# Half 1's softmax on a Trainium2 core: exponentials, sums and reciprocals issued one mixing round later

## The chip, the cores and the metric

The kernel runs on one core of one Trainium2 chip. Five engines work side by side, each with its own queue of instructions that it takes in order: TensorE (PE in the profile; its weight loads are PEld), VectorE (DVE), ScalarE (ACT), GpSimd (POOL) and SyncE (SP), which here issues most of the transfers. They wait for each other through semaphores. The metric is the device time of one execution in microseconds (us).

## The reference

The input `x` has 2048 tokens of 512 values, in bf16. It is normalised per token (`xn`), and two branches are computed from `xn` and added to `x`. Constants are cut out below.

```python
def _A_ref(x, wqkv, wo):                 # attention: 32 heads of 16, 8 taps, 2 tokens apart
    q, k, v = split(x @ wqkv)
    idx = pos[:, None] - 2 * arange(8)[None, :]
    logits = einsum('bhsd,bhswd->bhsw', q, k[idx]) * Dh ** -0.5
    logits = where(idx >= 0, logits, -1e9)
    attn = softmax(logits, axis=-1)      # over the 8 taps
    o = einsum('bhsw,bhswd->bhsd', attn, v[idx])
    return merge_heads(o) @ wo

def _B_ref(x, w_in, w_sp, b_sp, w_out):  # gated mixing over tokens
    z = gelu(x @ w_in)                   # 1376 columns
    z1, z2 = z[..., :688], layernorm(z[..., 688:])
    g = einsum('ts,bsf->btf', w_sp, z2) + b_sp[None, :, None]
    return (z1 * g) @ w_out

xn = layernorm(x)
return x + _A_ref(xn, A_wqkv, A_wo) + _B_ref(xn, B_w_in, B_w_sp, B_b_sp, B_w_out)
```

## The kernel before

The 2048 tokens are 16 tiles of 128. For the attention they are also two halves of 1024 (`hb` 0 and 1). Within a half, the 128 partitions hold 32 heads for each of four token groups, and 256 tokens of a group lie along a row. The order of the work is written out by hand: instructions stand in each engine's queue in the order in which the program issues them, and a transfer goes into the queue of the engine that issues it.

The first part (to about 67 us of the profile) normalises `x`, computes the `z2` half of the GELU for all tiles (line 241 on TensorE, 248 on ScalarE), and q, k and v. VectorE multiplies q by shifted k (`products`, line 344) and folds the channels (`fold`, 351); TensorE sums over them with a selection matrix (`head_sums`, 363), and ScalarE writes the logits to `a_sb` (`reduce_heads`, `reduce_two`: lines 369 and 375). `a_sb` holds 8 taps by 512 columns per partition: columns 0 to 255 are half 0, the others half 1.

**A softmax** of one half has five steps. `softmax_top` takes the maximum over the taps and subtracts it (VectorE, lines 382 to 385). `softmax_exp` is one ScalarE instruction on the whole half (388). `softmax_sums` adds the eight taps in three VectorE instructions (393 to 395) into the scratch tile `s4`. `softmax_recip` makes the reciprocal of the sums on ScalarE as Exp of minus Ln (399 and 400) into `r1`. `softmax_norm` multiplies the half by it on VectorE (404). ScalarE loads a table of functions (ACT_TABLE_LOAD) where the next instruction's function is not in the one at hand; a load carries the line of the instruction that it serves.

**The mixing rounds** are the second part. Round `j` has `mix(j)`, 32 matmuls of a row tile of `w_sp` with all of `z2` (line 576), whose result `pg` ScalarE evicts with the bias to `gs` (579), and `z1_tile(j)`, eight matmuls into `pz` (588), which ScalarE evicts through the GELU to `z1b` (592). From round 4 on, `pg` and `pz` come from one pool of two buffers (`ps_a`; the call `bank_pair(name, j > 3)` excludes the other). So the `pg` of a round can start only when `gs` has emptied the `pg` of the round before, and the same holds for `pz`. `mix` also issues the transposing load of `w_sp` for round `j + 5` on SyncE (411; `wspT` has five buffers). `gate_out(j)` multiplies `gs` by `z1` on VectorE (597), and SyncE sends the product through a transposing transfer into `uT` (598). `z1b` and `gs` have three buffers each.

**VectorE's own stream** runs beside these rounds. `av_ops` is a generator: for each quarter of 128 columns it multiplies `v` by the weights in four products (657), adds them (662, 664) and writes the quarter of `op` (666). After two quarters, which are half 0, it calls `softmax_norm(1)`, and goes on with half 1. `vector_work(4.6)` takes instructions from it until their stated times exceed 4.6 us. So a round of the loop from 691 on issues, in this order: `mix`, `z1_tile`, some of the products, and `gate_out(j - 1)`, with the steps of half 1's softmax at places fixed by `j`.

**The end.** `out_b` multiplies `uT` by `w_out` (line 746, six matmuls a tile), `out_a` multiplies `op` by `w_o` in row-tiled matmuls (755, 56 for each quarter `jj`), both into `po`; `store` adds `x` on VectorE (762) and SyncE writes the tile out. Fourteen of a head's 16 channels go through `op`; the two others are copied into unused rows of `uT` (`op_rest`, line 646, for half 1 from ScalarE's queue).

Of the kernel before, what the change touches and what calls it, by code (L numbers as in the profile page):

```python
# [47 lines left out]
def kernel(  # L48
# [328 lines left out]
    def softmax_top(hb):  # L377
        l = lg[hb]
        if hb == 0:
            V.tensor_tensor(l[0:32, :, 0:HALO], l[0:32, :, 0:HALO], mask[:], ALU.add)  # L380
        m4 = s4[:, 0].bitcast(BF16).rearrange("p a (b t) -> p (a b) t", b=2)
        V.tensor_tensor(m4, l[:, 0:4, :], l[:, 4:8, :], ALU.max)
        V.tensor_tensor(m4[:, 0:2, :], m4[:, 0:2, :], m4[:, 2:4, :], ALU.max)
        V.tensor_tensor(m4[:, 0, :], m4[:, 0, :], m4[:, 1, :], ALU.max)
        V.tensor_tensor(l, l, m4[:, 0, :].unsqueeze(1).broadcast_to([P, W, TG]), ALU.subtract)

    def softmax_exp(hb):
        A.activation(lg[hb], lg[hb], ACT.Exp)

    def softmax_sums(hb):  # L390
        hsl = slice(hb * TG, (hb + 1) * TG)
        halves = [a_sb[:, w:w + 4, hsl].rearrange("p (a b) t -> p a b t", b=2) for w in (0, 4)]
        V.tensor_tensor(s4[:], halves[0], halves[1], ALU.add)
        V.tensor_tensor(s4[:, 0], s4[:, 0], s4[:, 1], ALU.add)
        V.tensor_tensor(s4[:, 0, 0], s4[:, 0, 0], s4[:, 0, 1], ALU.add)

    def softmax_recip(hb):

        A.activation(s4[:, 0, 0], s4[:, 0, 0], ACT.Ln)
        A.activation(r1[:], s4[:, 0, 0], ACT.Exp, scale=-1.0)  # L400
# [171 lines left out]
    def mix(j):  # L572
        pg = bank_pair("pg", j > 3)
        for k in range(NT):
            for hh in range(2):
                PE.matmul(pg[:, hh, 0:FHALF], wsps[j][:, k, :], z2[:, k, hh * FHALF:(hh + 1) * FHALF],  # L576
                          start=(k == 0), stop=(k == NT - 1))
        gs = gsp.tile([P, 2, FHALF], BF16, name="gs")
        A.activation(gs[:], pg[:, :, 0:FHALF], ACT.Identity, bias=b_col[:, j:j + 1])  # L579
        if j + 5 < NT:  # L580
            load_wsp(j + 5)
        gss[j] = gs

    def z1_tile(j):
        pz = bank_pair("pz1", j > 3)
        for hh in range(2):
            for kc in range(C):
                PE.matmul(pz[:, hh, 0:FHALF], xnT[:, kc, j * P:(j + 1) * P],  # L588
                          w_z1[:, kc, hh * FHALF:(hh + 1) * FHALF],
                          start=(kc == 0), stop=(kc == C - 1))  # L590
        z1 = z1b[j % 3]
        A.activation(z1[:, 0:FH].rearrange("p (a b) -> p a b", a=2), pz[:, :, 0:FHALF], ACT.Gelu_apprx_tanh)  # L592
        z1s[j] = z1

    def gate_out(j):
        gs, z1 = gss.pop(j), z1s.pop(j)
        V.tensor_tensor(z1[:, 0:FH], gs[:].rearrange("p a b -> p (a b)"), z1[:, 0:FH], ALU.mult)
        SP.dma_start_transpose(uT[:, :, j * P:(j + 1) * P], z1[:])
# [43 lines left out]
    def op_rest(hb, q):  # L642

        for k in range(NG):
            for e in range(2):
                q.dma_start(uT[64 + 32 * e:96 + 32 * e, MCH - 1, hb * SB + k * TG:hb * SB + (k + 1) * TG],
                             op[32 * k:32 * k + 32, DHA + e, hb * TG:(hb + 1) * TG])
# [26 lines left out]
    def vector_work(us):  # L674
        while us > 0:
            t = next(work, None)
            if t is None:
                return
            us -= t
# [4 lines left out]
    def load_xr(jj):  # L684
        xr = xrp.tile([P, NG, D], BF16, name="xr")
        SP.dma_start(xr[:], x_g[jj // 2, jj % 2])
        xrs.append(xr)
# [3 lines left out]
    for j in range(4, NT):  # L691
        if j > 4:
            mix(j)
            z1_tile(j)
        if j == 8:
            softmax_recip(1)
        vector_work(4.6)
        if j == 6:
            softmax_top(1)
            softmax_exp(1)  # L700
        if j == 7:
            softmax_sums(1)
        gate_out(j - 1)
        if j == 5:
            SP.dma_start(wout[:, 0:MCH - 1, :], B_w_out[0:(MCH - 1) * P, :].rearrange("(m p) n -> p m n", p=P))
            SP.dma_start(wout[0:FTAIL, MCH - 1, :], B_w_out[(MCH - 1) * P:FH, :])
            for e in range(2):
                SP.dma_start(wout[64 + 32 * e:96 + 32 * e, MCH - 1, :],
                             A_wo.rearrange("(h d) n -> d h n", d=DH)[DHA + e])
        if 6 <= j < 10:  # L710
            k = j - 6
            SP.dma_start(wo_r[32 * k:32 * k + 32, :, :], A_wo.rearrange("(h d) n -> h d n", d=DH)[:, 0:DHA, :])
        if 11 <= j < 13:
            load_xr(j - 11)
        if j == 13:
            op_rest(0, SP)
# [96 lines left out]
```

## Time and profile before

| | |
|---|---|
| median of three runs | 201.62 us (200.99 to 202.24) |
| the profiled execution | 201.13 us, its span 199.4 us |
| granted TensorE clock in the span | 1.0 |
| mixing matmuls, line 576 | 512, mean 309 ns |
| products of VectorE, line 657 | 16, mean 2287 ns |
| the exponential, line 388 | 2 (one a half), mean 1911 ns |
| a table load on ScalarE | 1283 ns each, on every line |
| Ln and Exp of the reciprocals, lines 399 and 400 | 2 each, mean 417 and 418 ns |
| `gs`, line 579; GELU of `z1`, line 592 | 16 each, mean 832 and 744 ns |

The durations come from the one profiled execution. "Idle before" in a row is the time in which the engine stood still ahead of the instruction, followed by what released it. A group such as "x32" in the timeline is a run of like instructions that are merged: its first start and the time to the end of the last. Busy time in four stretches of the mixing rounds (from, to; then busy us and number of instructions for each engine, granted clock, mean busy share of the DMA engines, GB/s):

```profile
105.00:115.00 10.00, 10.00 (x71) 6.69 (x70) 9.86 (x9) 4.05 (x5) 0.00 (x0) 1.00 0.93 192
115.00:125.00 10.00, 9.39 (x66) 6.20 (x64) 9.86 (x9) 6.71 (x8) 0.00 (x0) 1.00 0.93 178
125.00:135.00 10.00, 10.00 (x70) 6.70 (x69) 9.96 (x7) 6.25 (x8) 0.00 (x0) 1.00 1.06 190
135.00:145.00 10.00, 10.00 (x71) 6.72 (x69) 9.93 (x8) 1.82 (x4) 0.00 (x0) 1.00 0.94 172
```

The columns of engines are PE, PEld, DVE, ACT and POOL. The mixing matmuls of rounds 5 to 9 start at 98.36, 104.20, 110.04, 116.64 and 122.47 us.

### The profile page before, as it was taken

What the parts mean: (1) busy time and instruction counts of PE and PEld (TensorE: products, weight loads), DVE (VectorE), ACT (ScalarE), POOL (GpSimd) and SP (SyncE); (2) the same over time, 40 slices, a digit from 0 to 9 for tenths busy, and PEclk for the clock granted to TensorE, in tenths of its full rate; (3) what the DMA queues carried; (4) which work ended last, traced back from release to release, by engine and by line L of the source; (5) the groups of instructions that cost most, each with busy time, mean ns of one, the idle gap of its engine ahead of it and who ended that gap; (6) DMA issues with size and microseconds to landing.
All of it is one profiled execution on the core that took longest, in us unless ns stands there. A gap on an engine that the chain in (4) does not pass through costs nothing.

```text
span 199.4 us, 3851 instructions
## 1 busy us (share of the span) xinstructions
PE 194.2 (97%) x1558; PEld 120.0 (60%) x1564; DVE 178.7 (90%) x208; ACT 105.0 (53%) x151; POOL 18.5 (9%) x65
## 2 busy tenths in 40 slices
PE   7999999999999999999999989999999999999994
PEld 7655555556666666666566656666666664444442
DVE  4899979999999999999999999999999999954083
ACT  4778987668898999496632575932133330000000
POOL 3045640002220020200100000000000000000000
PEclk9999999999999999999999999999999999999999
DMA  6984834998999239999899898999864222017632
GB/s 166 322 288 81 185 72 89 163 260 181 186 188 190 38 32 210 241 218 130 183 198 169 210 207 166 180 181 193 169 153 136 58 41 43 0 43 194 219 120 90
DMA packets 68770, 30.86 MB, mean 155 GB/s; under 512 B 57248, under 2 KB 67344, under 8 KB 68624
## 3 DMA queue, kind: packets, MB, share of 16 engines
q1 hardware_dynamic: 66976, 25.24, 58.3%
q0 software_dynamic: 1360, 5.24, 14.2%
q8 instruction: 12, 0.20, 0.4%
q10 hardware_dynamic: 416, 0.14, 0.3%
q14 instruction: 6, 0.05, 0.1%
HBM read 9.79 MB, written 2.10 MB: 60 GB/s over the span
## 4 chain that ended last, share of the span: by engine, by line
DVE 44%; PE 44%; issue 6%; POOL 3%; ACT 2%; DVEq 0%; ACTq 0%
PE pg L576 19%; DVE pr L344 15%; PE po L746 10%; PE po L755 6%; DVE pr L351 6%; PE pz L588 5%; DVE stats L197 2%; DVE pw L657 2%; DVE pw L662 2%; DVE qk L344 2%; DVE z L276 2%; PE idle L102 2%; DVE xn L202 1%; PE pzb L241 1%; DVE zst L259 1%
## 5 line engine op out<-in xcount | busy, mean ns | idle before, releaser
L576 PE MATMUL pg<-z,wspT 128*128 128x344 bf16 x512 | 77.1, 309 | 0.6 <-ACT gs L579 0.6
L576 PEld LDWEIGHTS <-wspT 128*128 128x128 bf16 x512 | 50.0, 98 | 25.7 <-issue 1.2
L657 DVE TENSOR_TENSOR pw<-vp,a_sb 128x4096 bf16<-128x4096 bf16 x16 | 36.3, 2287 | 0.1
L579 ACT ACTIVATE gs<-pg,b_col 128x688 bf16<-128x688 f32 x16 | 13.3, 832 | 38.7 <-PE pg L576 38.7
L344 DVE TENSOR_TENSOR pr<-qk 128x8192 bf16<-128x8192 bf16 (+1 forms) x8 | 30.9, 3882 | 0.0
L588 PE MATMUL pz<-w_z,xnT 128*128 128x344 bf16 x128 | 21.3, 309 | 0.0
L241 PE MATMUL pzb<-w_z,xnT 128*128 128x344 bf16 x128 | 19.8, 309 | 0.2 <-ACT xnT L226 0.2
L746 PE MATMUL po<-wout,uT 128*128 128x512 bf16 x88 | 19.3, 379 | 0.2 <-issue 0.2
L662 DVE TENSOR_TENSOR pw<-pw 128x4096 bf16<-128x4096 bf16 x8 | 18.3, 2289 | 0.1
L241 PEld LDWEIGHTS <-xnT 128*128 128x128 bf16 x128 | 12.4, 98 | 6.7 <-ACT xnT L226 0.4
L588 PEld LDWEIGHTS <-xnT 128*128 128x128 bf16 x128 | 12.4, 98 | 6.3 <-issue 0.3
L294 ACT CAST qk<-pq 128x1024 bf16<-128x1024 f32 x12 | 12.1, 1012 | 5.8 <-PE pq L291 5.8
L351 DVE TENSOR_TENSOR pr<-pr 128x2048 bf16<-128x2048 bf16 (+1 forms) x10 | 15.1, 1538 | 0.1
L746 PEld LDWEIGHTS <-uT 128*128 128x128 bf16 x90 | 8.7, 98 | 10.7 <-issue 0.4
L316 PE MATMUL pv<-xnT,wv 128*32 128x512 bf16 x256 | 14.4, 380 | 0.0
L592 ACT ACTIVATE z1b<-pz 128x688 bf16<-128x688 f32 x16 | 11.9, 744 | 4.0 <-PE pz L588 3.9
L762 DVE TENSOR_TENSOR ot<-po,xr 128x512 bf16<-128x512 f32 x15 | 9.5, 685 | 4.0 <-PE po L755 2.6
L248 ACT ACTIVATE z<-pzb 128x688 bf16<-128x688 f32 x16 | 11.8, 740 | 1.7 <-PE pzb L241 1.6
L291 PE MATMUL pq<-xnT,wk 128*128 128x512 bf16 x47 | 12.3, 379 | 0.1
L755 PE MATMUL po<-wo_r,op 32*128 32x512 bf16 x224 | 12.3, 374 | 0.0
L316 PEld LDWEIGHTS <-wv 128*32 128x32 bf16 x256 | 9.5, 139 | 4.5 <-issue 0.3
L291 PE MATMUL pq<-xnT,wq 128*128 128x512 bf16 x46 | 12.0, 379 | 0.1
(101 smaller groups left out, 202.0 us busy)
## 6 DMA issues: line engine op xcount, KB each, us to landing
pr<-pr POOLq DMA_DIRECT2D x4, 1024.0 KB, 9.6
xr<-in_A_x_dram SPq DMA_DIRECT2D x4, 512.0 KB, 4.5
out_dram<-ot SPq DMA_DIRECT2D x15, 128.0 KB, 1.7
wo_r<-in_A_wo_dram SPq DMA_DIRECT2D x4, 448.0 KB, 4.9
xq<-in_A_x_dram SPq DMA_DIRECT2D x2, 512.0 KB, 7.4
qk<-qk POOLq DMA_DIRECT2D x1, 1024.0 KB, 12.4
w_z<-in_B_w_in_dram SPq DMA_DIRECT2D x2, 344.0 KB, 4.4
w_z<-in_B_w_in_dram SPq DMA_DIRECT2D x1, 688.0 KB, 5.2
```

The lines of the kernel that those rows point to most:

```text
L241: PE.matmul(pz[:, hh, 0:FHALF], xnT[:, kc, i * P:(i + 1) * P], w_z2[:, kc, hh * FHALF:(hh + 1) * FHALF], start=(kc == 0), stop=(kc == C - 1))
L291: PE.matmul(pq[:, s, :], wqk_v[s][:, kc, c], xnT[:, kc, tsl], start=(kc == 0), stop=(kc == C - 1))
L316: PE.matmul(pv[32 * k:32 * k + 32, dd, :].rearrange("p (b t) -> p b t", b=NB), wv_v[:, kc, 2 * d2 + dd, :], xnT_g[:, kc, :, k, :], start=( ...
L344: V.tensor_tensor(pr[:, :, cs, :], qk[hb][:, cs, 0, HALO:HALO + SB].unsqueeze(1).broadcast_to([P, 2, n, SB]), shifted(qk[hb][:, cs, 1, off ...
L351: V.tensor_tensor(pr[:, :, 0:n, :], pr[:, :, 0:n, :], pr[:, :, n:2 * n, :], ALU.add)
L576: PE.matmul(pg[:, hh, 0:FHALF], wsps[j][:, k, :], z2[:, k, hh * FHALF:(hh + 1) * FHALF], start=(k == 0), stop=(k == NT - 1))
L579: A.activation(gs[:], pg[:, :, 0:FHALF], ACT.Identity, bias=b_col[:, j:j + 1])
L588: PE.matmul(pz[:, hh, 0:FHALF], xnT[:, kc, j * P:(j + 1) * P], w_z1[:, kc, hh * FHALF:(hh + 1) * FHALF], start=(kc == 0), stop=(kc == C - 1))
L657: V.tensor_tensor(pw[:], shifted(vp[:, :, hb, off:off + P]), a_sb[:, 2 * p:2 * p + 2, osl].unsqueeze(2).broadcast_to([P, 2, DH, P]), ALU.mult)
L662: V.tensor_tensor(pws[p - 1][:], pws[p - 1][:], pw[:], ALU.add)
L746: PE.matmul(pos[jj, k][:], uT[:, m, i * P:(i + 1) * P], wout[:, m, :], start=first and m == 0, stop=not first and m == MCH - 1)
L755: PE.matmul(pos[jj, k][:], op[32 * k:32 * k + 32, d, jj * P:(jj + 1) * P], wo_r[32 * k:32 * k + 32, d, :], start=first and d == 0, stop=(n ...
```

## The change

The exponentials of half 1 move from the end of round 6's VectorE work to round 7, behind that round's `mix` and `z1_tile` and ahead of its products; the sums move from round 7 to round 8, and the reciprocals from round 8 to round 9. `softmax_top(1)` stays in round 6 and `softmax_norm(1)` stays in `av_ops`. No instruction is added, removed or altered.

```diff
@@ -692,13 +692,14 @@
         if j > 4:
             mix(j)
             z1_tile(j)
-        if j == 8:
+        if j == 7:
+            softmax_exp(1)
+        if j == 9:
             softmax_recip(1)
         vector_work(4.6)
         if j == 6:
             softmax_top(1)
-            softmax_exp(1)
-        if j == 7:
+        if j == 8:
             softmax_sums(1)
         gate_out(j - 1)
         if j == 5:
```

## The prediction

> **What bounds the kernel now.** First the page's head and its busy times, then the chain of waits in order of time, then the timeline around the one place where that chain leaves TensorE.
>
> ```profile
> span 199.4 us, 3851 instructions
> PE 194.2 (97%) x1558; PEld 120.0 (60%) x1564; DVE 178.7 (90%) x208; ACT 105.0 (53%) x151; POOL 18.5 (9%) x65
> ```
>
> TensorE is busy for 97% of the span, so the question is where the other 3% lies after the start. The chain answers it (start, length, what):
>
> ```profile
> 113.96 0.97 ACT a_sb L388
> 114.93 0.85 issue
> 115.77 0.82 ACT gs L579
> 116.60 0.04 issue
> ...
> 163.52 10.31 PE po L746 x47
> 173.83 12.20 PE po L755 x224
> ```
>
> From 116.64 us to the last rows the chain stays on TensorE. Before that it runs over VectorE (the maxima) and ScalarE: the exponential of line 388 and then `gs`, the eviction of line 579. The timeline of those microseconds:
>
> ```profile
> 110.04 4.83 PE L576 MATMUL pg<-z,wspT 128*128 128x344 bf16 x32
> ...
> 112.66 1.28 ACT L388 ACT_TABLE_LOAD   x1 [1.63 <-DVE a_sb L385]
> ...
> 113.96 1.91 ACT L388 ACTIVATE a_sb<-a_sb 128x2048 bf16<-128x2048 bf16 x1
> ...
> 114.70 1.33 PE L588 MATMUL pz<-w_z,xnT 128*128 128x344 bf16 x8
> ...
> 115.77 0.82 ACT L579 ACTIVATE gs<-pg,b_col 128x688 bf16<-128x688 f32 x1
> ...
> 116.64 4.83 PE L576 MATMUL pg<-z,wspT 128*128 128x344 bf16 x32 [0.61 <-ACT gs L579]
> ```
>
> Round 7's 32 mixing matmuls end near 114.9 us, but ScalarE is in the exponential until 115.87, so `gs` 7 starts at 115.77 (the rows overlap a little). Two buffers serve `pg` and `pz`; round 8's `pg` needs the one that `gs` 7 empties. In other rounds `gs` starts 0.20 us after the first `pz` matmul (138.80 and 139.00), here 1.07 us after it. Starts of mixing rounds lie 5.84 us apart (104.20, 110.04) and 5.83 (116.64, 122.47); from 110.04 to 116.64 it is 6.60. The stall costs 6.60 - 5.835 = 0.77 us; the 0.61 us shown is less because modelled matmul ends overlap the next start by 0.16 (138.80 + 1.33 against 139.97).
>
> **The exponential.** It is removed from behind `z1` 6, where it had to wait 1.63 us for the maxima, and put behind `z1` 7. With the stall gone, round 7's `pz` stays at 114.70, `gs` 7 runs at 114.90 to 115.73, and `z1` 7 starts 1.22 us after `gs`, as in round 6 (109.07, 110.29), and takes 0.74: it ends at 116.86. The maxima are done since 112.6, so the table load starts at once: 116.88 + 1.30 (load, 112.66 to 113.96) + 1.91 = 120.09. Round 8's `pz` starts at 114.70 + 5.835 = 120.54 and `gs` 8 can start at 120.74. ScalarE is free 0.65 us earlier, so the path pays nothing. If this cover were gone, what is late is again `gs`, behind the exponential on ScalarE, and TensorE behind it. The number of table loads stays five: one before the exponential, one for the GELU after it, one each for Ln and Exp of the reciprocals, one for the next GELU (in round 10, as now in round 9). The first GELU's load falls in round 8: 121.57 + 0.02 + 2.04 (load to end of `z1`, 116.61 to 118.65) ends at 123.63, and its `pz` buffer is wanted at 126.37.
>
> A table load's price decides this window. Here each load lasts 1.28 us and begins and ends within 0.02 us of its neighbours. [...]
>
> **Sums.** Three VectorE adds (1.22, 0.69 and 0.43 us; 118.59 to 120.91 with overlaps, 2.32) go from ahead of `gate_out(6)` to ahead of `gate_out(7)`. Between lie a product and an add of 2.29 us each and the gate. VectorE's total is unchanged: gate 6 runs 2.32 us earlier, at 118.59 (its inputs are ready since 111.03), the product at 119.0, the add at 121.3, the sums at about 123.6 to 125.9, and gate 7 again at 125.87. The new wait (sums on exponential, 123.6 against 120.09) has 3.5 us of room; behind it in VectorE's queue stand gate 7 and the products. On SyncE gate 6's transpose comes out earlier; ahead of it stands the load of `wspT` 12, issued once mixing round 7 is over. Loads run five rounds ahead, so I cost both at nothing. DMA engines are 93% busy or more from 95 to 135 us, so an earlier transpose can delay a neighbour, but what it could delay is five rounds from its use.
>
> **Reciprocals.** Two loads, Ln and Exp move from behind `z1` 8 to behind `z1` 9. The rows of before:
>
> ```profile
> 123.48 1.28 ACT L399 ACT_TABLE_LOAD   x1
> ...
> 126.50 0.42 ACT L400 ACTIVATE r<-s 128x256 bf16<-128x256 f32 x1
> 127.34 0.83 ACT L579 ACTIVATE gs<-pg,b_col 128x688 bf16<-128x688 f32 x1 [0.42 <-PE pg L576]
> ```
>
> They take 3.44 us (123.48 to 126.92) and leave 0.42 us before the next `gs`. One round later they meet the same space: `gs` 9 at 126.57, `z1` 9 ends at 128.53, 128.55 + 3.44 = 131.99, `gs` 10 at 132.41. The sums are there at about 125.9, 2.6 us early. Who reads the result is the normalisation on VectorE, at 137.22: 5.2 us late enough. If the cover of 0.42 went, `gs` 10 would wait behind them.
>
> **The end.** The remaining 0.77 us must get past the output. VectorE has hardly a pause from 95 to 175 us and doesn't finish earlier: its last write of `op` ends at 174.97. The third block of 56 row-tiled matmuls (line 755) first needs buffers that VectorE's stores free, the fourth needs that last write, near 182. VectorE now waits for TensorE ahead of these stores:
>
> ```profile
> 176.99 2.48 DVE L762 TENSOR_TENSOR ot<-po,xr 128x512 bf16<-128x512 f32 x4 [2.02 <-PE po L755]
> ```
>
> So 1.25 of the 2.02 us remain. The ScalarE queue's copies of `op` to `uT` start at 175.00 whatever TensorE does and are out by 181.2, wanted from 185.4. The whole 0.77 comes through.
>
> **Sum.** The profiled execution took 201.13 us (span 199.4 and 1.7 around it): 201.13 - 0.77 = 200.36. It lies 0.49 below the median of three, 201.62; on that basis 200.85, and I state 200.8. Bounds of the stall's worth: 0.61 us (the idle shown) to 0.87 (how late `gs` started).
>
> **Rival 1, the gain is swallowed.** One row says that line 755's first weight load waited for VectorE:
>
> ```profile
> 98.36 4.49 PEld L576 LDWEIGHTS <-wspT 128*128 128x128 bf16 x32 [0.42 <-issue]
> ...
> 173.76 11.77 PEld L755 LDWEIGHTS <-op 32*128 32x128 bf16 x224 [0.42 <-DVE pw L664]
> ...
> 185.95 8.75 PEld L746 LDWEIGHTS <-uT 128*128 128x128 bf16 x42 [0.42 <-issue]
> ```
>
> If true, TensorE arrives 0.77 earlier and waits for the same VectorE add: only some 0.07 is left, 201.55. Against it: the code reads only the first quarter of `op` there, written by 116.5; and two other switches between tiled and whole matmuls show the same 0.42 us with nobody to wait for. It looks like the switch, and the add's end like coincidence. 9%.
>
> **Rival 2, slower: VectorE waits for the exponential.** The exponential writes half 1 of `a_sb`; the product at 116.39 reads half 0, but comes after it in the program. Were the two halves of a row taken as one, the product would wait until 120.09, 3.70 us; before, the exponential had ended by then, so the page can't show it. VectorE would end its products at 178.67, its four stores run to 181.15, and the third block starts then instead of at 173.83 + 6.10 - 0.77 = 179.16: 1.99 lost, 1.22 net, 202.8. It decides once VectorE is over some 1.7 us late (1.25 and the 0.46 between the last store and the third block). Without any cover it would be 3.70 - 0.77 = 2.93, 204.6. Against it: the same kind of pair at 95 to 100 us.
>
> ```profile
> 95.53 4.49 DVE L657 TENSOR_TENSOR pw<-vp,a_sb 128x4096 bf16<-128x4096 bf16 x2
> ...
> 98.13 1.08 ACT L369 ACTIVATE a_sb<-pl 128x512 bf16<-128x512 f32 x2
> ...
> 99.08 1.04 ACT L375 ACTIVATE a_sb<-plb 128x1024 bf16<-128x1024 f32 x1
> ```
>
> The ScalarE writes of half 1 come first in the program, yet the products ran without waiting. 8%.
>
> **Rival 3, ScalarE runs out of room.** Suppose that in the new places each table switch holds ScalarE for a second load's length, 1.28 us. Then the exponential ends at 121.37, 0.63 after `gs` 8 is due, and the two switches in round 9 overrun by 2.56 - 0.42 = 2.14. Each loses TensorE that much less 0.09, the usual room between `gs` (139.83, and 0.05 to hand over) and the next round (139.97): 0.54 + 2.05 = 2.59, net 1.82, 203.4. It decides from 0.65 us more in round 8, 0.42 in round 9. The last group of rows denies it: load, Ln, load and Exp stand end to end. 2%. [...]
>
> **How the numbers follow.** Forecast 78%, rivals 9, 8 and 2%, something unseen 3%. Range 200.0 to 202.1: the fastest run less the gain is 200.22, the slowest 201.47, and rival 1 reaches 202.17 with the slowest; outside lie rivals 2 and 3 and scatter. About 1% (2.0 us) is what a measurement can tell from no change. The forecast is 0.4%, so within 1% has 91%; faster 4%, from scatter; slower 5%, from the far ends of rivals 2 and 3 and the unseen.
>
> **What would show it.** The exponential right behind `z1` 7, over before `gs` 8; 5.83 us between the mixing starts at 110.04 and about 115.88, and in all later rounds; no pause in VectorE's row near 116; Exp of the reciprocals over by 132.4; line 755 starting near 173.1. I am wrong if any later `gs` starts late, if VectorE pauses, or if line 755 still starts at 173.8.

## The result, and the profile after

The changed kernel took 200.72 us in the median of 17 runs (200.36 to 201.87), the kernel before 201.47 (200.99 to 202.24, 17 runs): ratio 0.9966, 95% interval 0.9951 to 0.9982. That is 0.7 us faster, inside the range (200.8 us was forecast) and inside the 1% that was called no change. A second measurement of it, told below, gave 0.9965 (0.9949 to 0.9981).

Two lines of the changed kernel's page, its head and the shares of the chain of waits by engine:

```profile
span 198.9 us, 3852 instructions
...
PE 92%; DMA 4%; DVE 1%; SPq 1%; issue 1%
```

The same shares before:

```profile
DVE 44%; PE 44%; issue 6%; POOL 3%; ACT 2%; DVEq 0%; ACTq 0%
```

VectorE and TensorE had 44% of the chain each, since it left TensorE at round 8's start for `gs`, the exponential and the maxima, and ran over VectorE for most of what came before. Now nothing in the mixing rounds leads away from TensorE. The timeline of the changed kernel at that place (start, length, engine and line, operation, idle before):

```profile
115.09 0.83 ACT L579 ACTIVATE gs<-pg,b_col 128x688 bf16<-128x688 f32 x1 [3.88 <-PE pg L576]
...
116.06 4.83 PE L576 MATMUL pg<-z,wspT 128*128 128x344 bf16 x32
...
116.53 2.28 DVE L657 TENSOR_TENSOR pw<-vp,a_sb 128x4096 bf16<-128x4096 bf16 x1
117.07 1.28 ACT L388 ACT_TABLE_LOAD   x1
118.36 1.91 ACT L388 ACTIVATE a_sb<-a_sb 128x2048 bf16<-128x2048 bf16 x1
...
119.16 2.28 DVE L657 TENSOR_TENSOR pw<-vp,a_sb 128x4096 bf16<-128x4096 bf16 x1
...
120.93 0.83 ACT L579 ACTIVATE gs<-pg,b_col 128x688 bf16<-128x688 f32 x1 [0.65 <-PE pg L576]
```

`gs` 7 starts as soon as its matmuls are over, round 8 follows without a pause, and the exponential lies in ScalarE's gap behind `z1` 7, with 0.65 us to spare. Mixing round 7 starts at 110.22 in this execution, so 7 to 8 takes 5.84 us instead of 6.60. The gain arrives undiminished at the output: from round 6's start (104.39; 104.20 before) to the first row-tiled weight load is 68.79 us (173.18) against 69.56 (173.76). The span is only 0.5 us shorter since this execution was already 0.19 us later at round 6's start. From there to the end of VectorE's last add is 91.99 us (to 196.38), against 92.76 before (to 196.96): 0.77 again. This stretch, which leaves out the first 104 us and their scatter, is given for some of the experiments too. Two rows of the changed kernel's output stage:

```profile
173.18 11.77 PEld L756 LDWEIGHTS <-op 32*128 32x128 bf16 x224 [0.42 <-issue]
...
176.41 2.48 DVE L763 TENSOR_TENSOR ot<-po,xr 128x512 bf16<-128x512 f32 x4 [1.31 <-PE po L756]
```

The 0.42 us ahead of the first row-tiled load is still there, but VectorE is no longer named, and TensorE came 0.58 us earlier while VectorE's add ended 0.13 later, at 173.84. VectorE's wait for TensorE ahead of the stores went from 2.02 to 1.31 (1.25 was forecast).

### The profile page after: what moved, and what is told of

Its sections match the earlier page's. It is cut to its first block, busy times and chain, and to the rows that moved or that the text cites. A ratio compares the mean times of both kernels' runs of the same rounds, so it can differ in the third digit from the quotient of the medians.

```text
span 198.9 us, 3852 instructions
## 1 busy us (share of the span) xinstructions
PE 194.0 (98%) x1558; PEld 119.9 (60%) x1564; DVE 178.5 (90%) x208; ACT 105.1 (53%) x151; POOL 18.5 (9%) x65
## 4 chain that ended last, share of the span: by engine, by line
PE 92%; DMA 4%; DVE 1%; SPq 1%; issue 1%
PE pg L576 38%; PE pq L291 10%; PE po L747 10%; PE pzb L241 10%; PE pz L588 9%; PE pv L316 7%; PE pq L303 3%; PE po L756 3%; DMA out_dram<-ot 2%; DMA w_z<-in_B_w_in_dram 2%; PE pl L363 1%; DVE ot L763 1%; PE po L729 1%; PE pt L224 0%; SPq L182 0%
```

## The experiments

Diffs are against the changed kernel, except where another is named. All were timed with the kernel before on the same chip; the ratios are to it.

**Only the exponential moved.**

```diff
-        if j == 9:
+        if j == 8:
             softmax_recip(1)
...
-        if j == 8:
+        if j == 7:
             softmax_sums(1)
```

> Only the exponential is moved to round 7; sums stay in round 7, reciprocals in round 8. Theory (the gain is ScalarE's room ahead of gs, and all three steps must move for it): the stall at round 8's mixing start goes (-0.77 us), but VectorE's sums now wait for the exponential (about 120.27 on the changed kernel's clock, 1.5 us after VectorE gets there at 118.8), and Ln and Exp of the reciprocals start behind z1 8 with its own GELU table load, at about 124.17: 124.17 + 3.44 = 127.6 against gs 9 due at 126.76. gs 9 some 0.84 late, TensorE loses about 0.75, VectorE's 1.5 us lies within its room of 1.31 + 0.46 us at the end. Sum: about the time before, 201.5 us, ratio 1.000. Rival (the exponential's move carries the gain and the other two moves are idle): 200.7 us, ratio 0.9965, no late gs in round 9.

Measured: 201.79 us, 1.0008 (0.9989 to 1.0026). From its timeline, VectorE's sums, then ScalarE's last Exp of the reciprocals and `gs` 9, then mixing round 10:

```profile
120.17 1.23 DVE L393 TENSOR_TENSOR s<-a_sb 128x1024 f32<-128x1024 bf16 x1 [1.47 <-ACT a_sb L388]
```

```profile
127.06 0.42 ACT L400 ACTIVATE r<-s 128x256 bf16<-128x256 f32 x1
127.39 0.82 ACT L579 ACTIVATE gs<-pg,b_col 128x688 bf16<-128x688 f32 x1
```

```profile
128.26 4.83 PE L576 MATMUL pg<-z,wspT 128*128 128x344 bf16 x32 [0.51 <-ACT gs L579]
```

Round 8 starts on time, and the stall is back two rounds later: 6.51 us between the starts of rounds 9 and 10 (121.75, 128.26), 0.68 lost where 0.75 was expected. So the exponential's move brings nothing while the reciprocals stay in round 8: the GELU's table load now falls into that round, and Ln and Exp no longer fit behind it. The sums waited 1.47 us for the exponential, but in the profiled execution that cost nothing more: from round 6's start to the end it took 92.66 us, 0.67 over the changed kernel's 91.99. Whether the sums' move is needed at all is not shown, as no run left out that one alone.

**Reciprocals in round 8, behind the sums.**

```diff
-        if j == 9:
-            softmax_recip(1)
...
         if j == 8:
             softmax_sums(1)
+            softmax_recip(1)
```

> Exponential and sums as changed, reciprocals one round earlier: in round 8 behind the sums. Theory (a late gs is paid by TensorE and reaches the end one for one): the sums end at about 126.1, so table load, Ln, table load and Exp run to 126.1 + 3.44 = 129.55, gs 9 is due at 126.76 and is 2.75 late; less 0.09 of room TensorE loses 2.66 us: 200.72 + 2.66 = 203.4 us, ratio to before 1.0094. Rival (VectorE's chain sets the end, TensorE's stall is absorbed behind it): the part beyond 0.1 us is hidden, 200.8 us.

Measured: 202.13 us, 1.0029 (1.0011 to 1.0048). Slower than the changed kernel, but by half of what was expected. ScalarE's rows of this run, then TensorE's:

```profile
124.85 1.28 ACT L399 ACT_TABLE_LOAD   x1
126.84 0.42 ACT L399 ACTIVATE s<-s 128x256 f32<-128x256 f32 x1 [0.70 <-DVE s L395]
```

```profile
129.76 4.83 PE L576 MATMUL pg<-z,wspT 128*128 128x344 bf16 x32 [1.20 <-ACT gs L579]
```

The table load for Ln did not wait for the sums, only Ln did. The expectation had counted that load behind the sums: 2.66 - 1.28 = 1.38, and the trace shows 7.20 - 5.835 = 1.37 lost (122.56 to 129.76). Against the changed kernel the medians' ratios give 0.0063 x 201.5 = 1.3 us. So this stall did reach the end one for one; only its size was misjudged.

**The exponential back in round 6, sums and reciprocals left where the change put them.**

```diff
-        if j == 7:
-            softmax_exp(1)
...
         if j == 6:
             softmax_top(1)
+            softmax_exp(1)
```

> The exponential goes back to round 6 behind the maxima; sums stay in round 8 and reciprocals in round 9. Theory (the whole gain is the stall of gs 7 behind the exponential; the sums' and reciprocals' places cost and bring nothing by themselves): the 0.77 us stall at round 8's start is back, 6.60 us between the mixing starts, 201.47 us, ratio 1.000. Rival (part of the gain comes from gate 6 and its transpose running 2.3 us earlier, or from the emptier round 8): between 200.7 and 201.4 us with that stall in place.

Measured: 201.45 us, 0.9998 (0.9982 to 1.0014). The mixing row of round 8:

```profile
117.08 4.83 PE L576 MATMUL pg<-z,wspT 128*128 128x344 bf16 x32 [0.59 <-ACT gs L579]
```

Round 7 started at 110.49, so 6.59 us again, and from round 6's start to the end it took 92.74 us (92.76 before). The earlier gate 6 and the emptier round 8 bring nothing by themselves.

**ScalarE's gap filled.**

```diff
             softmax_exp(1)
+            for _ in range(4):
+                A.activation(r1[:], xnT[:, 0, 0:TG], ACT.Exp)
```

> The changed kernel with four more Exp activations of 256 columns (0.42 us each, some 0.1 of it overlapping the next) behind the moved exponential; their result is overwritten by the reciprocals. Theory (ScalarE has 0.65 us of room there and no more): 4 x 0.33 to 0.42 = 1.3 to 1.7 us more, gs 8 starts 0.65 to 1.0 late, TensorE loses 0.6 to 0.95: 201.3 to 201.7 us, ratio to before about 1.000, the gain is given back in the round after. Rival (ScalarE at 53% busy has enough slack and a later gs is made up): 200.7 us.

Measured: 201.38 us, 1.0011 (0.9988 to 1.0035). The four took 1.75 us, `gs` 8 came at 121.62, and rounds 8 and 9 started at 115.84 and 122.49: 6.65, so 0.81 lost. ScalarE is busy 53% of the changed kernel's span, but its room in this round ends at 0.65 us.

**The maxima a round earlier instead of the exponential later**, a diff against the kernel before:

```diff
+        if j == 6:
+            softmax_exp(1)
         if j == 8:
             softmax_recip(1)
         vector_work(4.6)
-        if j == 6:
+        if j == 5:
             softmax_top(1)
-            softmax_exp(1)
```

> The kernel before with the maxima one round earlier (round 5) and the exponential behind z1 6 in round 6; sums and reciprocals stay in rounds 7 and 8. Theory (what matters is that the exponential finds its data ready when ScalarE falls idle behind z1, not that it is late): the exponential ends about 114.4, gs 7 is due at 115.1, no stall; Ln and Exp in round 8 end about 126.3 with gs 9 due at 126.8. As fast as the changed kernel: 200.7 us, ratio to before 0.9965. Rival (only the later round has room for it): the stall stays, 201.5 us.

Measured: 200.59 us, 0.9955 (0.9935 to 0.9976). The rows of the exponential and of `gs` 7:

```profile
112.69 1.91 ACT L388 ACTIVATE a_sb<-a_sb 128x2048 bf16<-128x2048 bf16 x1
115.25 0.83 ACT L579 ACTIVATE gs<-pg,b_col 128x688 bf16<-128x688 f32 x1 [0.65 <-PE pg L576]
```

The same 0.65 us of room one round earlier. What counts is that the data are there when ScalarE falls idle behind `z1`. It was timed again beside the changed kernel:

> Maxima one round earlier, exponential behind z1 6, beside the changed kernel. Theory (both only remove the same stall): equal within 0.2 us. Rival (the first measurement's 0.9955 against 0.9966 is a real gain of 0.2 us): 0.2 us faster or more.

> The changed kernel itself, beside the next three on the same chip, as their measure: ratio to before 0.9966 as before.

Measured: 0.9966 (0.9939 to 0.9993) and 0.9965 (0.9949 to 0.9981), 200.47 and 200.60 us. No difference shows, and from round 6's start to the end both profiled executions took 91.99 us; the first 0.9955 was scatter.

**VectorE's room at the end.** The `op` write of half 1's first quarter done twice, 1.22 us more:

```diff
-                V.tensor_tensor(op[:, :, osl], pws[0][:, 0], pws[0][:, 1], ALU.add)
+                for _ in range(2 if (hb, q) == (1, 0) else 1):
+                    V.tensor_tensor(op[:, :, osl], pws[0][:, 0], pws[0][:, 1], ALU.add)
```

> The changed kernel with one write of op (line 666, 1.22 us) done twice, in half 1 behind the normalisation: VectorE's stream ends 1.22 us later. Theory (VectorE has 1.31 us of room ahead of the first stores and another 0.55 between the last of them and TensorE's third block of row-tiled matmuls): nothing is lost, 200.7 us, ratio to before 0.9965, and VectorE's wait ahead of the first store shrinks from 1.31 to about 0.1 us. Rival (VectorE, 90% busy and without a pause from 95 to 175 us, bounds the kernel together with TensorE): 1.2 us lost, 201.9 us, ratio 1.0025.

Measured: 201.30 us, 0.9988 (0.9964 to 1.0013), which decides nothing. Round 6's start and the last add in the profiled execution, which took 201.37 us:

```profile
105.20 4.83 PE L576 MATMUL pg<-z,wspT 128*128 128x344 bf16 x32
...
196.78 0.42 DVE L732 TENSOR_TENSOR ot<-po,rest 128x256 bf16<-128x256 f32 x1 [0.21 <-PE po L730]
```

From the one to the end of the other is 92.00 us, as in the changed kernel. What this execution has over the changed kernel's 200.60 us it had at round 6's start, which is 0.81 us later (104.39 there) and ahead of the edit. Once more, beside the changed kernel:

> VectorE's stream 1.22 us longer, again, since the first measurement (0.9964 to 1.0013) leaves both no loss and half a microsecond open. Theory (room of 1.86 us): the same time as the changed kernel beside it, within 0.2 us. Rival (a room of 1.31 us is eaten now and then by scatter in the start): 0.3 to 0.6 us slower than the changed kernel.

Measured: 201.42 us (200.31 to 202.54), 1.0000 (0.9979 to 1.0022), 0.8 us over the 200.60 beside it. The median misses the theory's "within 0.2 us", although the fastest run equals the changed kernel's. That run is the profiled one, at 200.31; it shows no stall on TensorE and takes 91.99 us from round 6's start to the end. What it does show is VectorE's last stretch. First the changed kernel beside it, then this run:

```profile
188.99 0.69 DVE L778 TENSOR_TENSOR rest<-po,xr 128x512 f32<-128x512 f32 x1 [7.14 <-DMA xr<-in_A_x_dram]
189.60 3.09 DVE L763 TENSOR_TENSOR ot<-po,xr 128x512 bf16<-128x512 f32 x5
```

```profile
190.27 0.69 DVE L779 TENSOR_TENSOR rest<-po,xr 128x512 f32<-128x512 f32 x1 [8.62 <-DMA xr<-in_A_x_dram]
190.88 4.26 DVE L764 TENSOR_TENSOR ot<-po,xr 128x512 bf16<-128x512 f32 x7
```

Seven stores now stand end to end and are over at 195.14, where VectorE's last adds begin (195.06): no room is left, though nothing is lost yet. The cause lies two queues away. With VectorE's last `op` write, the copies to `uT` on ScalarE's queue start 1.13 us later (176.21 against 175.08); SyncE's first output store, whose data were ready at 176.84, goes out at 178.62, its wait put down to those copies; and the two loads of `x` behind the stores move from 180.78 and 183.54 to 182.05 and 184.59. Whether this is the loss in the other runs was tried by taking these loads out of the way, with the doubled write left in:

```diff
-    xrp = ctx.enter_context(tc.tile_pool(name="xrp", bufs=2, reuse_waits="tile", **right))
+    xrp = ctx.enter_context(tc.tile_pool(name="xrp", bufs=3, reuse_waits="tile", **right))
...
-        if 11 <= j < 13:
+        if 11 <= j < 14:
             load_xr(j - 11)
...
-            load_xr(jj + 2)
+            if jj == 0:
+                load_xr(3)
```

> VectorE's stream 1.22 us longer as before, but x for the third output quarter is loaded in round 13 and for the fourth 2.5 us earlier (three buffers instead of two). Theory (the loss of 0.6 to 0.8 us with 1.22 us more came from a third wait: the ScalarE queue's copies start later, SyncE's first output store and the two loads of x behind it come 1.0 to 1.3 us later, and the remainder and seven stores of VectorE then end without any room): the remainder runs near 187 us instead of 190.3, VectorE's last stores follow TensorE again, and the time is the changed kernel's, ratio to before 0.9965. Rival (the loss lies elsewhere, in the scatter of the start or ahead of the third block): 0.999 to 1.000 again.

Measured: 200.52 us, 0.9957 (0.9936 to 0.9978), with the 1.22 us still in it. This is no version that beats the changed kernel: the intervals overlap. The `rest` row ran at 188.28, later than the expected 187 but 2.0 us earlier than without the edit, and VectorE's last stores wait for TensorE again (0.56 to 0.60 us each). The median is the one that the theory expected, but the cause is not shown. In all three profiled executions with the 1.22 us, round 6's start to the end takes 91.99 or 92.00 us, so no trace shows the third wait costing time here. The 0.6 to 0.8 us of the two medians can as well be the scatter ahead of round 6, and the earlier loads were not tried without the 1.22 us.

**4.57 and 2.44 us more on VectorE.** One product of half 1 done three times, and the `op` write done three times.

```diff
-                    V.tensor_tensor(pw[:], shifted(vp[:, :, hb, off:off + P]),
...
+                    for _ in range(3 if (hb, q, p) == (1, 0, 0) else 1):
+                        V.tensor_tensor(pw[:], shifted(vp[:, :, hb, off:off + P]),
...
```

> The changed kernel with one product of VectorE (line 657, 2.29 us) done three times instead of once, in half 1 behind the normalisation: VectorE's stream ends 4.57 us later. Theory (room 1.31 + 0.55 us, then one for one): TensorE's third block of row-tiled matmuls waits for the stores, 4.57 - 1.86 = 2.7 us lost: 203.4 us, ratio to before 1.0100. Rival A (co-bound, no room): 4.6 us lost, 205.3 us. Rival B (the stores are not on the path): 200.7 us.

Measured: 205.11 us, 1.0155 (1.0119 to 1.0192), in six runs. The profiled execution is the longest of them, 206.47 us. TensorE's first matmul of the third block, from the timeline, and the stretches around it (from, to; busy us and number for PE, PEld, DVE, ACT, POOL; granted clock; DMA share; GB/s):

```profile
181.67 0.37 PE L757 MATMUL po<-wo_r,op 32*128 32x512 bf16 x1 [1.06 <-DVE ot L764]
```

```profile
184.00:185.00 1.00, 1.00 (x16) 0.51 (x12) 1.00 (x3) 0.00 (x0) 0.00 (x0) 0.50 0.70 215
187.00:188.00 1.00, 1.00 (x24) 0.50 (x20) 0.00 (x0) 0.00 (x0) 0.00 (x0) 0.86 0.56 45
```

The block ran freely from 183.46, some 2.85 us after the second block ended (180.61): the wait for the stores is as expected, 2.7. What was not expected comes behind it, and is read in the granted clock, the column after POOL: it was half (0.50 from 184 to 187, 0.93 and 0.86 in the microseconds beside) for 3.4 us, which is 1.7 us of work lost. From the first row-tiled weight load to the last stage's, TensorE took 16.89 us in this execution (174.39 to 191.28), against 12.19 in the changed kernel: 4.70 lost, of which the two account for 4.4. The half clock did not come in every run, however. The mean granted clock is 0.990 to 0.992 in four of the six, and 0.999 in the two others (203.53 and 204.83 us). The fastest, without it, is near the theory's 203.4, and the median mixes both kinds.

```diff
-                V.tensor_tensor(op[:, :, osl], pws[0][:, 0], pws[0][:, 1], ALU.add)
+                for _ in range(3 if (hb, q) == (1, 0) else 1):
+                    V.tensor_tensor(op[:, :, osl], pws[0][:, 0], pws[0][:, 1], ALU.add)
```

> The same write of op done three times: VectorE's stream 2.44 us longer. Theory (room 1.31 + 0.55 = 1.86 us, then one for one, and a pause of TensorE that short leaves its clock alone): 0.6 us over the changed kernel, a gap of 0.6 us ahead of the third block, granted clock 1.0 throughout. Rival (any pause there costs the half clock that followed the 2.9 us pause in the run with 4.57 us): 1.5 us or more over the changed kernel.

Measured: 201.58 us, 1.0017 (0.9992 to 1.0042), 1.0 us over the changed kernel beside it. TensorE lost 0.8 us ahead of and in the third block (12.99 us from the first row-tiled weight load to the last stage's, 12.19 in the changed kernel), at full clock (1.00 from 170 to 198); the stores behind `rest` (191.59), which stand end to end, put VectorE's last adds off by another 0.2 (11.20 us from the last stage's first weight load to the end, against 11.01). Here the late loads of `x` do cost time. Both theories missed this second part.

## Why the prediction was right

- **The stall and its size.** 0.77 us was read from the distance of mixing starts, not from the 0.61 us of idle shown. The trace after gives 0.77 (69.56 - 68.79), the measured ratio 0.0034 x 201.5 = 0.7. That the stall is the whole gain is shown both ways: it returns with the exponential alone put back, and it vanishes as well when the maxima come early.
- **The exponential's new place.** It ended at 120.27; 120.09 was forecast, on a clock that runs 0.18 us later in this execution. Room before `gs` 8: 0.65, as worked out. With 1.75 us of work put there, TensorE lost 0.81.
- **Sums and reciprocals.** Sums at 123.68 to 126.09 (forecast 123.6 to 125.9), the last Exp over at 132.18 (131.99), `gs` 10 with 0.42 us idle ahead of it, as forecast. That the reciprocals have to move for the gain to stay, though their move brings nothing alone, was not said in the prediction; the exponential's move alone gave nothing.
- **The GELU's load** was put at 121.59, right behind `gs` 8. It ran at 122.12, after the matmuls of `pz`: this load waited 0.36 us for them, as its activation does (see the last section). It cost nothing.
- **Rival 1** fell: line 755's counterpart starts 0.58 us earlier with the same 0.42 us ahead of it. It starts 0.66 us before the add (173.84) ends that was named before, so that add was not awaited; the name was coincidence.
- **Rival 2** fell: a product that reads half 0 started at 119.16, in the middle of the exponential's 118.36 to 120.27, without idle time. The room of "some 1.7 us" in its price fits what the third block showed: 2.44 us more on VectorE cost TensorE 0.8 there. But it overlooked the loads of `x`, which added 0.2 behind that.
- **Rival 3** fell: in every run the second load follows Ln, and Exp that load, within 0.02 us. A switch that holds ScalarE for a second load's length, 1.28 us, shows in none.

## What to carry to other kernels

When a result buffer is emptied by an engine's strict queue, look at what stands in the queue ahead of the eviction and still waits for data: an instruction belongs where its inputs are ready and the gap behind it is longer than it is with its table loads. Price such a stall by the distance between starts of like rounds, and check the gap of each later round that inherits a load or a table switch, since moving one step alone can shift the stall by two rounds (here from round 8's start to round 10's, 0.68 us). Where the runs scatter ahead of the change, compare traces from a common point behind the scatter to the end. Room at the end of a stream is the smallest over all that follows from it, transfers on other queues included (here the loads of `x`, 0.2 us).

## What the runs showed of the hardware

- **Behind one pause TensorE's clock was halved.** With 4.57 us more on VectorE, after 2.85 us with only three lone matmuls (180.61 to 183.46) the granted clock was 0.93 in the microsecond from 183, 0.50 in the three from 184 and 0.86 in that from 187: half speed for 0.14 + 3 + 0.28 = 3.4 us. Two of this kernel's six runs show no such drop in their mean clock (0.999; 0.990 to 0.992 in the four others). The profiled executions with shorter pauses at a mixing start have a mean clock of 0.999 to 1.0: 0.51 us with the exponential alone moved, 0.59 with it back in round 6, 1.20 with the reciprocals in round 8. That it was the pause that halved the clock was not shown by itself.
- **Two table loads, two ways of waiting.** Before the change the exponential's load stood still until the maxima were there (1.63 us); in the run with the reciprocals in round 8 Ln's load was over 0.70 us before the data came and only Ln waited. The traces tell the two apart. Before line 388's load, ScalarE's queue holds a wait as an instruction of its own (in the row below, the second one, of half 1, at 112.6 us; the load starts at 112.66). Line 399 has none in either of the two kernels (its view lists two loads and two activations, no more), and in the run with the reciprocals in round 8 only Ln itself waits. The GELU's load at 122.12 in the changed kernel also stands behind such a wait (120.93 to 122.10). Why one line gets the separate wait and the other not was not tried.

```profile
L388 ACTq EVENT_SEMAPHORE  x2: 17/17/17, 75.1 to 112.6; - x2
```

- **The spread of the runs comes in part from the first 10 us.** TensorE waited for the first weights (`w_z`) 0.33 us in the changed kernel's profiled execution, 0.63 in that with the reciprocals in round 8, 0.99 and 1.16 in those with 1.22 us and 4.57 us more on VectorE. Round 6's mixing started at 104.39, 105.06, 105.20 and 105.60 in them, long before the edits of the latter two. Behind that start the time hardly scatters: from round 6's start to the end of VectorE's last add it is 91.99 or 92.00 us in all seven profiled executions of the changed kernel, of the one with the early maxima and of those with 1.22 us more.
